# Layer norm, attention with one key head, and a gate, on one core: statistics of one token tile on ScalarE, and an instruction order recorded anew

## The chip, the core and the metric

The kernel runs on one core of a Trainium2 chip. Its engines run their own instruction streams side by side and wait for one another through semaphores: TensorE (PE, with its weight loads shown apart as PEld), VectorE (DVE), ScalarE (ACT), GpSimd (POOL) and SyncE (SP), which here only starts DMAs. TensorE writes to PSUM, a small memory in banks of 128 x 512 fp32; all other data is in SBUF. The metric is the time of one execution on the device in microseconds; a comparison goes by the median of several executions.

## What is computed

For 2048 tokens of width 512, with 32 query heads of width 16 that share one key head and one value head:

```python
xn = (x - mean(x)) / sqrt(var(x) + 1e-5)             # per token
q, k, v = xn @ wq, xn @ wk, xn @ wv                   # 32 heads of 16; one k, one v
s = concat_heads(softmax(q k^T / 4) v) @ wo           # no mask
g = silu(silu(xn @ w1) @ w2)                          # 512 -> 1792 -> 512
out = x + s * g
```

The largest part is the softmax: 32 heads x 2048 x 2048 scores, each of which needs an exponential.

## The kernel before

**Tiles and blocks.** Tokens are cut into 16 tiles of 128 and four chunks of 512. The attention is cut into 32 groups: a group is one chunk of 512 queries and four heads. In a group there are 16 key tiles, and for each key tile four score blocks (one a head) of 128 keys x 512 queries; in all 32 x 16 x 4 = 2048 blocks. A score is a matmul with 16 of the array's rows in use (32 by place), so up to four heads' blocks run side by side in "row" mode; the value products, the projections and the dense layers run in "column" mode, four matmuls of 32 columns side by side (a "quad").

**Two ways to an exponential.** ScalarE takes two blocks at once: scores go to one of two double banks (`psA`), one `Exp` over 128 x 1024 reads them and writes `pa_sb` (line 601), and each block then needs one value product into `psO` (line 723). VectorE takes single blocks from three banks (two halves of `psD`, and `psF`): it makes the bit pattern of a bf16 power of two by adding an offset and rounding to int16 (`ph_sb`, line 639), and GpSimd adds two further offsets to it as packed 64-bit integers (line 664), so that three weighted value products together are near the exponential. A free part of `x_sb` serves as a fourth buffer for these, which is why rows with `x_sb<-psD` are the same work. A block on VectorE so costs three value products where one on ScalarE costs one. The gates' `Tanh` (line 1039) is ScalarE's as well; the group's normalisation (lines 794 to 821), the evacuations of projections and the dense layer are VectorE's.

**The order.** Nothing is ordered by hand after the front. A recorder, class `Sched`, runs when the kernel is built: `op` appends an instruction to an engine's queue, works out its semaphore waits from the keys that it reads and writes, and keeps a model of each engine's clock from costs given with the operations (an operation on GpSimd or VectorE without a cost counts as 0.4 us). The main loop asks that model at each step what to issue next: it fills the time before ScalarE's next pair of scores is needed with value products (`emit_PV`), projection and dense jobs (`emit_job`, bank `psF`, by due times), the front's remaining work (`emit_front`) or zero matmuls that keep TensorE busy (`filler`), and then issues the pair (`score_run`) with single blocks for VectorE beside it (`fill_D`). `advance_v` orders VectorE's tasks. The loop's numbers (how late a bank may come free, how many quads ahead, the share of activity under which fillers are put in, how many buffers may be held) are chosen by stretch: the model's time of ScalarE, divided into stretches of 12 us, picks a letter of `PLAN`, and the letter a row of `RULES`. So a changed cost or rule in one place reorders everything that comes after it.

**The front.** Tiles 0 to 3 are loaded first: 0 and 2 by SP's queue, 1 and 3 by ScalarE's, then wk, a part of wq, tiles 4 to 7, the rest of wq, wv, and the other tiles on SP. While 15 zero matmuls run, VectorE makes statistics of the four tiles (`stats`, line 379, one `bn_stats` each) and aggregates them to mean and variance (`aggr`, line 382). ScalarE takes the square root (`rstd_sqrt`, line 393) and loads the exponential's table; VectorE takes the reciprocal and normalises. Transposes, the first part of the keys and the first queries follow, and the first scores. For the later chunks GpSimd makes the reciprocal root (`rstd_pow`, lines 386 and 388). Two lines of it:

```python
        for t in tiles(0):
            stats(t)
```

**The end.** The last group is done in two halves of 256 queries, then come the last projection, the gate and the last stores.

Of the kernel before, what the change touches and what calls it, by code (L numbers as in the profile page):

```python
# [5 lines left out]
ACT = mybir.ActivationFunctionType  # L6
ALU = mybir.AluOpType
AX = mybir.AxisListType
FP32 = mybir.dt.float32
# [4 lines left out]
P = 128  # L14
DH = 16
NQ = 512
# [180 lines left out]
def bass_recurrent_scan__grouped_kv_mqa__dense_activation_silu__prompt_kernel(  # L197
# [13 lines left out]
    S, D = xf.shape  # L211
    F = B_w1.shape[1]
# [9 lines left out]
    NPA = 11  # L222
# [4 lines left out]
    NWARM = 15  # L227
    NWARM2 = 0
    NWARM3 = 2
    NFRONT = 12  # L230
    AGE2, AGE_ST, FIRST, FRONT_D, FRONT_K, SHORT, ST_EARLY, Q_ACT = 12.0, 1.5, 9.4, 1, 4, 0, 3, 1
    KEEP, ENDQ, ROUND, MAXJOB, AHEAD, Q_EARLY = 0.65, 12, 3.0, 2, 3, 0.18
    LEAD, LEAD_END, SLIP, AGE, AGE1, MARGIN = 3, 1, 0.2, 2.0, 1.2, 0.0
    HALF_LO, HALF_HI = 1, 3
    EV = "vava"
    PVWAIT, FKEEP = 0.2, 0.75
    NPAIR, LEAD_PAIR = 1, 1


    STRETCH = 12.0  # L240
    PLAN = (
        "AAAOFFAAJFNIAOEJAAGAKAALBACLAMFGKLFPNLFANFAEAAAQHAAODBA"
    )
    RULES = dict(
        A=(0.2, 3.0, 0.65, 10, 1.2, 2.0, 0, 12, 0.2, 3, 3, 0.0),
        B=(0.1, 3.0, 0.65, 10, 1.2, 2.0, 0, 12, 0.2, 3, 3, 0.0),
        C=(0.15, 3.0, 0.65, 10, 1.2, 2.0, 0, 12, 0.2, 3, 3, 0.0),
        D=(0.3, 3.0, 0.65, 10, 1.2, 2.0, 0, 12, 0.2, 3, 3, 0.0),
        E=(0.2, 3.0, 0.65, 11, 1.2, 2.0, 0, 12, 0.2, 3, 3, 0.0),
        F=(0.2, 3.0, 0.65, 10, 1.2, 2.0, 4, 12, 0.2, 3, 3, 0.0),  # L250
        G=(0.2, 3.0, 0.65, 10, 1.2, 2.0, 8, 12, 0.2, 3, 3, 0.0),
        H=(0.2, 3.0, 0.65, 10, 1.2, 2.0, 0, 24, 0.2, 3, 3, 0.0),
        I=(0.2, 3.0, 0.65, 7, 1.2, 2.0, 8, 12, 0.1, 3, 3, 0.0),
        J=(0.25, 3.0, 0.65, 8, 1.2, 2.0, 4, 12, 0.2, 3, 3, 0.0),
        K=(0.2, 3.0, 0.65, 7, 1.2, 2.0, -4, 12, 0.2, 3, 3, 0.04),
        L=(0.2, 3.0, 0.65, 10, 2.0, 3.0, 0, 12, 0.2, 3, 3, 0.04),
        M=(0.1, 3.0, 0.65, 10, 2.0, 3.0, 0, 12, 0.2, 3, 3, 0.0),
        N=(0.2, 3.0, 0.65, 10, 1.2, 1.0, 8, 12, 0.2, 3, 3, 0.04),
        O=(0.15, 3.0, 0.5, 10, 1.2, 2.0, 0, 12, 0.2, 2, 3, 0.0),
        P=(0.3, 3.0, 0.7, 10, 1.2, 2.0, 0, 6, 0.2, 3, 3, 0.0),  # L260
        Q=(0.25, 3.0, 0.65, 9, 1.2, 2.0, 0, 12, 0.2, 4, 3, 0.0),
    )
    NF, F_FROM, F_LEFT, F_LATE, DENSE_END, HOLD, F_BEHIND = 14, 0.05, 9, 3, 0.97, 10, 0

    with ExitStack() as es:
        def sb(name, shape, dt=BF16):
            return es.enter_context(nc.sbuf_tensor(name, shape, dt))

        x_sb = sb("x_sb", [P, NT, D])
        xn_sb = sb("xn_sb", [P, 8, D])  # L270
        on_sb = xn_sb
        xnT_sb = sb("xnT_sb", [P, NDC, S])
        wq_sb = sb("wq_sb", [P, NDC, D])
# [15 lines left out]
        t_sb = sb("t_sb", [P, 2, NQ])  # L289
# [6 lines left out]
        mv_sb = sb("mv_sb", [P, NT, 2], FP32)  # L296
# [41 lines left out]
        for j in range(NPH + 1):  # L338
# [11 lines left out]
        op("gp", lambda e: e.tensor_copy(wkp4[:, :, :, 0:DH], wkn_sb[:, :, :].unsqueeze(2).to_broadcast([P, NDC, 4, DH])),  # L350
           reads=["wkn", "wkp"], writes=["wkp"])

        def load_w1():
            op("sp", lambda e: e.dma_start(w1_sb[:], B_w1.rearrange("(dc p) f -> p dc f", p=P)), writes=["w1"], lane="lw1", cost=7.0)

# [19 lines left out]
        def tiles(c):  # L375
            return range(4 * c, 4 * c + 4)
# [7 lines left out]
        def rstd_pow(c):  # L384
            sl = slice(4 * c, 4 * c + 4)
            op("gp", lambda e: e.tensor_scalar(rstd_sb[:, sl], mv_sb[:, sl, 1], LN_EPS, None, op0=ALU.add),
               reads=[("mv", t) for t in tiles(c)], writes=[("rstd", c)])
            op("gp", lambda e: e.tensor_tensor(rstd_sb[:, sl], rstd_sb[:, sl], mhalf_sb[:, :], ALU.pow),  # L388
               reads=[("rstd", c), "mhalf"], writes=[("rstd", c)])

        def rstd_sqrt(c):
            sl = slice(4 * c, 4 * c + 4)
# [105 lines left out]
                   cost=0.155 + (b - a) * P / 960)  # L498

        warm(NWARM, psF[:, :], "F")  # L500
        for t in tiles(0):
            stats(t)
        for t in tiles(0):
            aggr(t)
        rstd_sqrt(0)
        for t in tiles(0):
# [79 lines left out]
        def held(key):  # L586
            return any(p["key"] == key for q in pend for p in q)
# [564 lines left out]
        def needed():  # L1152

            return K.act_end - 0.685 - MARGIN
# [47 lines left out]
        def target(t):  # L1202


            rel, need = max(release(), t), needed()
            if need <= rel:
                return rel
            used = [b for b in dst["fifo"]]
            idle = K.free["v"] + sum(0.6 for b in used)
            frees = [K.ready("pe", [], [b]) for b in BANKS if hold[b] is None]  # L1210
            f = min(frees) if frees else K.free["v"] + 0.65
            x = max(f, idle - 0.43)
            return min(max(rel, x), need) if x <= need + SLIP else need

        def score_run(t):
# [27 lines left out]
            if second:  # L1243
                ast["tile"] = None

        def fill_D(t, free):

            banks = sorted(free_banks(t + SLIP), key=lambda b: (b == "F", K.ready("pe", [], [b])))
            keep = 0
            if "F" in banks and jobs and behind(F_BEHIND) and next_job(t):  # L1250
# [36 lines left out]
        K.free["a"] = max(K.free["a"], FIRST - 0.3)  # L1287
        now, gp_end = 0.0, False
        while state["g"] < NGRP or front or jobs or jst["open"] or tasks:
            (SLIP, ROUND, KEEP, HOLD, AGES["gn1"], AGE, F_BEHIND, ENDQ, PVWAIT, LEAD, AHEAD, MARGIN) = \  # L1290
                RULES[PLAN[min(int(K.act_end / STRETCH), len(PLAN) - 1)]]
            t = max(now, min(K.pe_next("col"), K.pe_next("full")))
            if t > 2000.0:
                raise ValueError(f"the order does not end {state} {jobs[:3]} {jst} {tasks} {dst} {ast}")
# [45 lines left out]
            if more and not blocked:  # L1340
                idle = slots - did
                if idle > 0 and K.activity(max(t, K.pe_last + K.pe_len) + 0.216 * idle) < (FKEEP if front else KEEP):
                    filler(idle)
                score_run(t)
                now = 0.0
            elif not did:
                if dst["open"]:
                    fill_D(t, [0, 1, 2, 3])
                now = t + 0.05
            else:  # L1350
                now = 0.0
# [96 lines left out]
```

## Time and profile before

| | us |
|---|---|
| median of 3 executions | 671.5 (671.2 to 671.59) |
| the profiled execution | 673.14 |
| its span, first to last instruction | 670.3 |
| ScalarE busy | 657.9 (98%) |
| TensorE busy (matmuls) | 649.2 (97%) |
| VectorE busy | 599.9 (90%) |
| GpSimd busy | 375.0 (56%) |
| first `Exp` of scores starts | 10.59 |
| last `Exp` of scores ends | 663.1 |
| `Exp` of scores on ScalarE | 669, 1202 ns each, overlapping |
| blocks on VectorE | 710 (2048 less 2 x 669) |

A group of instructions is given as line, engine, operation, tile written and tile read, shapes, and count; then busy time, the mean in ns of one, and the idle time of the engine just before them with what ended most of it. Neighbouring instructions of an engine overlap, so a mean can be longer than the pace. The chain is the work that ended last, followed back from the last instruction to whatever released it. A row of the windows gives a stretch of time, the busy time and count of each engine, the granted clock of TensorE as a share of the full one, and the share and rate of DMA.

### The profile page before, as it was taken

To read this page: it belongs to the slowest core of one execution; us is meant where nothing else is said; L and a number is where in the kernel's file an instruction comes from. 1 tells how busy PE (TensorE), PEld (TensorE's weight loads), DVE (VectorE), ACT (ScalarE), POOL (GpSimd) and SP (SyncE) were. 2 spreads that over 40 slices of the span, in tenths; PEclk is the share of its full clock that TensorE was granted. 3 is DMA by queue.
4 is the path that set the end of the run, shared out by engine and by line. 5 is a ranking of instruction groups with operands and counts; after the bars stand their busy time and mean duration, and the time that the engine had idled before them with its cause. 6 is when DMAs were issued, how large, how long until landed. Compare 5 with 4: busy or idle time off the path is not lost.

```text
span 670.3 us, 18577 instructions
## 1 busy us (share of the span) xinstructions
PE 649.2 (97%) x8137; PEld 182.2 (27%) x8143; DVE 599.9 (90%) x1008; ACT 657.9 (98%) x755; POOL 375.0 (56%) x379
## 2 busy tenths in 40 slices
PE   8999999999999999999999999999999999999997
PEld 4422222222222222222222222222222222222222
DVE  7899889898888988999899889898899889888997
ACT  6999999999999999999999999999999999999997
POOL 3156546465565655555665566564565547656652
PEclk9999999899999999999999999999999999999999
DMA  6340000000000001000000000010000000000110
GB/s 174 139 147 1 2 2 1 2 1 2 2 1 2 1 18 34 17 2 2 1 2 2 1 2 2 1 34 17 18 2 1 2 2 1 2 2 1 34 33 31
DMA packets 12336, 12.48 MB, mean 19 GB/s; under 512 B 2528, under 2 KB 11744, under 8 KB 12256
## 3 DMA queue, kind: packets, MB, share of 16 engines
q1 hardware_dynamic: 11680, 10.78, 5.2%
q8 instruction: 63, 1.03, 0.6%
q10 hardware_dynamic: 576, 0.52, 0.2%
q14 instruction: 17, 0.14, 0.1%
HBM read 8.95 MB, written 2.10 MB: 16 GB/s over the span
## 4 chain that ended last, share of the span: by engine, by line
ACT 77%; PE 16%; DVE 6%; POOL 1%; DMA 0%; issue 0%; ACTq 0%
ACT pa_sb L601 72%; PE psA L571 5%; PE psO L723 5%; ACT t_sb L1039 5%; PE psF L363 4%; DVE ph_sb L639 1%; DVE stats_sb L379 1%; DVE xn_sb L400 1%; POOL rstd_sb L388 0%; PE psD L571 0%; DVE x_sb L639 0%; DMA x_sb<-in_A_x_dram 0%; PE psD L411 0%; DVE onb_sb L811 0%; PE psD L442 0%
## 5 line engine op out<-in xcount | busy, mean ns | idle before, releaser
L601 ACT ACTIVATE pa_sb<-psA 128x1024 bf16<-128x1024 f32 x669 | 636.5, 1202 | 3.2 <-PE psA L571 1.7
L664 POOL INT64_ADD ph_sb<-ph_sb x292 | 302.3, 1048 | 214.6 <-DVE ph_sb L639 214.4
L639 DVE TENSOR_SCALAR ph_sb<-psD 128x512 int16<-128x512 f32 x513 | 349.5, 692 | 40.1 <-PE psD L571 32.7
L723 PE MATMUL psO<-ph_sb,vaug_sb 128*32 128x512 bf16 x1758 | 218.3, 385 | 0.3
L723 PE MATMUL psO<-pa_sb,vaug_sb 128*32 128x512 bf16 (+1 forms) x1346 | 202.8, 383 | 0.6 <-DVE onb_sb L835 0.6
L571 PE MATMUL psA<-qT_sb,kTa_sb 32*128 32x512 bf16 x680 | 131.9, 384 | 4.5 <-ACT pa_sb L601 3.1
L571 PE MATMUL psA<-qT_sb,kTb_sb 32*128 32x512 bf16 x650 | 126.5, 386 | 7.0 <-ACT pa_sb L601 6.3
L571 PE MATMUL psD<-qT_sb,kTb_sb 32*128 32x512 bf16 x325 | 119.5, 385 | 1.0 <-DVE ph_sb L639 1.0
L571 PE MATMUL psD<-qT_sb,kTa_sb 32*128 32x512 bf16 x311 | 114.0, 384 | 0.0
L664 POOL INT64_ADD x_sb<-x_sb x62 | 64.3, 1049 | 44.9 <-DVE x_sb L639 44.9
L639 DVE TENSOR_SCALAR x_sb<-psD 128x512 int16<-128x512 f32 (+1 forms) x110 | 75.5, 691 | 11.7 <-PE psD L571 10.9
L571 PEld LDWEIGHTS psA<-qT_sb,kTa_sb 32*128 32x128 bf16 x680 | 32.0, 91 | 145.1 <-ACT pa_sb L601 131.2
L571 PEld LDWEIGHTS psA<-qT_sb,kTb_sb 32*128 32x128 bf16 x650 | 30.6, 91 | 144.7 <-ACT pa_sb L601 132.3
L363 PE MATMUL psF<-xnT_sb,w_sb 128*32 128x512 bf16 x896 | 69.6, 386 | 0.0
L363 PE MATMUL psF<-w_sb,u_sb 128*32 128x512 bf16 x896 | 69.2, 384 | 0.0
L723 PEld LDWEIGHTS psO<-ph_sb,vaug_sb 128*32 128x32 bf16 x1758 | 53.9, 95 | 51.2 <-issue 35.3
L723 PE MATMUL psO<-x_sb,vaug_sb 128*32 128x512 bf16 x372 | 65.9, 383 | 0.0
L723 PEld LDWEIGHTS psO<-pa_sb,vaug_sb 128*32 128x32 bf16 x1346 | 49.3, 95 | 43.5 <-issue 34.8
L1039 ACT ACTIVATE t_sb<-psF 128x512 bf16<-128x512 f32 x72 | 56.2, 781 | 0.0
L1071 DVE SCALAR_TENSOR_TENSOR u_sb<-t_sb,psF 128x512 bf16<-128x512 bf16 x56 | 38.2, 682 | 4.8 <-ACT t_sb L1039 3.6
L639 DVE TENSOR_SCALAR ph_sb<-psF 128x512 int16<-128x512 f32 x62 | 42.1, 680 | 0.0
L571 PEld LDWEIGHTS psD<-qT_sb,kTb_sb 32*128 32x128 bf16 x325 | 28.2, 91 | 2.4 <-DVE ph_sb L639 1.4
(125 smaller groups left out, 361.7 us busy)
## 6 DMA issues: line engine op xcount, KB each, us to landing
w_sb<-in_B_w_dram SPq DMA_DIRECT2D x2, 1792.0 KB, 8.9
x_sb<-in_A_x_dram SPq DMA_DIRECT2D x18, 128.0 KB, 2.3
out_dram<-ob_sb SPq DMA_DIRECT2D x14, 128.0 KB, 1.7
x_sb<-in_A_x_dram SPq DMA_DIRECT2D x3, 512.0 KB, 6.5
wop_sb<-in_A_wo_dram SPq DMA_DIRECT2D x1, 512.0 KB, 4.2
wq_sb<-in_A_wq_dram SPq DMA_DIRECT2D x1, 384.0 KB, 6.2
x_sb<-in_A_x_dram ACTq DMA_DIRECT2D x2, 128.0 KB, 2.8
kTb_sb<-kTa_sb SPq DMA_DIRECT2D x16, 16.0 KB, 1.8
```

The costliest lines, as they stand in the source:

```text
L363: r = e.matmul(bank[32 * i:32 * i + 32, :], lhsT=lhsT[:, 32 * i:32 * i + 32], rhs=rhs, start=start, stop=stop, tile_position=(0, 32 * i), ...
L379: op("v", lambda e: e.bn_stats(stats_sb[:, t, :], x_sb[:, t, :]), reads=[("x", t)], writes=[("st", t)], cost=0.687)
L400: op(eng, lambda e: e.tensor_scalar(xn_sb[:, t % 8, :], x_sb[:, t, :], mv_sb[:, t, 0:1], rstd_sb[:, t:t + 1], op0=ALU.subtract, op1=ALU.mult),
L571: return e.matmul(ap, lhsT=kT_sb[g % 2][32 * i:32 * i + 32, kt * P:(kt + 1) * P], rhs=qT_sb[32 * i:32 * i + 32, c % 2, g // 2, :], start=T ...
L601: d = op("a", lambda e: e.activation(pa_sb[:, sl, :], psA[k][:, :], ACT.Exp, scale=ESCALE), reads=["A%d" % k], writes=[("pa", sl)], cost=2 ...
L639: d = op("v", lambda e: e.tensor_scalar(ph_ap(0, sl, 512 * pos, 512 * pos + m), src, float(PH_ONE + PH_BIAS), 0.0, op0=ALU.add, op1=ALU.ma ...
L664: d = op("gp", lambda e, j=j: e.int64_add(ph_ap(j, sl, 0, 4 * NQ).bitcast(I64), ph_ap(0, sl, 0, 4 * NQ).bitcast(I64), PH_SHIFT[j] * 0x0001 ...
L723: r = e.matmul(psO[32 * i:32 * i + 32, cs], lhsT=vaug_sb[:, p["v"], p["kt"], :], rhs=p["ap"], start=s0, stop=s1, tile_position=(0, 32 * i) ...
L1039: op("a", lambda e: e.activation(t_sb[:, n % 2, :], bank_ap(b), ACT.Tanh, scale=0.5 if jb[0] == "h" else 0.25), reads=[b], writes=[("t", n ...
L1071: op("v", lambda e: e.scalar_tensor_tensor(out=dst, in0=t_sb[:, n % 2, :], scalar=1.0, in1=src, op0=ALU.add, op1=ALU.mult), reads=tk["read ...
```

## The change

Three things are changed.

The statistics of tile 1 go to ScalarE. `stats_act` first issues a square root of a constant, then a copy of the tile scaled by 1/512 whose sum is the mean, then a small copy that scales the mean by 512 to the power -1/2, then a square of (mean - x) scaled alike, whose sum is the variance. The other three tiles stay on VectorE.

The recorder is given 0.3 and 1.07 us for the two GpSimd operations of `rstd_pow` in place of 0.4 each.

The numbers per stretch are chosen anew: another `PLAN` (56 letters in place of 55), other `RULES` with two more columns, the letter now picked 0.35 us ahead, and `NFRONT` 16 in place of 12, which sets from what progress on projection and dense jobs are due. The two new columns are `AIM`, until now a fixed 0.43 in `target`, and `XGAIN`: where it is below 2, `extra_fill` runs after each `score_run` and issues one more block for VectorE if a bank comes free within 0.3 us and VectorE would by the model be spared more idle time than `XGAIN` plus the wait. It is below 2 in the letters I, J, K, O and R, which stand in 14 of the 56 places.

```diff
-    NFRONT = 12
+    NFRONT = 16
...
+    XHOLD, XTASK, XWAIT, XGAIN, XCOST, XOPEN, XBEH, AIM = 7, 0, 0.3, 9, 1.0, 0, 99, 0.43
...
-    STRETCH = 12.0
+    STRETCH, AHEAD_BY = 12.0, 0.35
     PLAN = (
-        "AAAOFFAAJFNIAOEJAAGAKAALBACLAMFGKLFPNLFANFAEAAAQHAAODBA"
+        "AAAJFHIPQRACARAAREKMLBPAHAOQDMDJAAJKHQGGQOFIRNIQFGGEMBBA"
     )
     RULES = dict(
-        A=(0.2, 3.0, 0.65, 10, 1.2, 2.0, 0, 12, 0.2, 3, 3, 0.0),
...
+        A=(0.2, 3.0, 0.65, 10, 1.2, 2.0, 0, 12, 0.2, 3, 3, 0.0, 9, 0.43),
...
+        J=(0.2, 3.0, 0.65, 10, 1.2, 2.0, 0, 12, 0.2, 3, 3, 0.0, 0.25, 0.43),
...
+        def stats_act(t):
+
+            r = D ** -0.5
+            op("a", lambda e: e.activation(scr_sb[:, 1:2], eps_sb[:, 0:1], ACT.Sqrt), reads=["eps"], writes=["scr1"], cost=4)
+            op("a", lambda e: e.activation(t_sb[:, 0, :], x_sb[:, t, :], ACT.Copy, scale=1.0 / D, accum_out=mv_sb[:, t, 0:1]),
+               reads=[("x", t)], writes=[("t", 0), ("mean", t)], cost=NQ)
+            op("a", lambda e: e.activation(nm_sb[:, 0:1], mv_sb[:, t, 0:1], ACT.Copy, scale=r), reads=[("mean", t)],
+               writes=["nm"], cost=4)
+            op("a", lambda e: e.activation(t_sb[:, 1, :], x_sb[:, t, :], ACT.Square, scale=-r, bias=nm_sb[:, 0:1],
+                                           accum_out=mv_sb[:, t, 1:2]),
+               reads=[("x", t), "nm"], writes=[("t", 1), ("mv", t)], cost=NQ)
...
-               reads=[("mv", t) for t in tiles(c)], writes=[("rstd", c)])
+               reads=[("mv", t) for t in tiles(c)], writes=[("rstd", c)], cost=0.3)
...
-               reads=[("rstd", c), "mhalf"], writes=[("rstd", c)])
+               reads=[("rstd", c), "mhalf"], writes=[("rstd", c)], cost=1.07)
...
-        for t in tiles(0):
+        stats_act(1)
+        for t in (0, 2, 3):
             stats(t)
-        for t in tiles(0):
+        for t in (0, 2, 3):
             aggr(t)
...
-            x = max(f, idle - 0.43)
+            x = max(f, idle - AIM)
...
+        def extra_fill():
+
+            t = K.pe_last + K.pe_len
+            if sum(held(("pa", k)) for k in range(NPA)) >= XHOLD or group_A() >= NGRP or (XOPEN and jst["open"]) or (XBEH < 99 and behind(XBEH)):
+                return
+            advance_v(t + 0.05)
+            vfree = K.free["v"] + 0.62 * len(dst["fifo"]) + sum(tk["cost"] for tk in tasks if XTASK and all(n in tok for n in tk["need"]) and K.ready("v", tk["reads"], tk["writes"]) < t + 0.6)
+            ride = max(needed(), t + 0.2) + 0.43
+            best = None
+            for b in BANKS:
+                if hold[b] is None and (b != "F" or not jobs or not behind(F_BEHIND) or not next_job(t)):
+                    r = max(t, K.ready("pe", [], [b]))
+                    gain = max(vfree, ride) - max(vfree, r + 0.43)
+                    if r <= t + XWAIT and gain > XGAIN + XCOST * (r - t):
+                        if best is None or r < best[0]:
+                            best = (r, b)
+            if best is None:
+                return
+            fill_D(best[0], [0, 1, 2, 3], [best[1]])
...
-        def fill_D(t, free):
+        def fill_D(t, free, only=None):
...
+            if only:
+                banks = only
...
-                RULES[PLAN[min(int(K.act_end / STRETCH), len(PLAN) - 1)]]
+                RULES[PLAN[min(int((K.act_end + AHEAD_BY) / STRETCH), len(PLAN) - 1)]]
...
                 score_run(t)
+                if XGAIN < 2:
+                    extra_fill()
```

More of the change, by code (lines that the diff above doesn't have):

```diff
@@ L237, in bass_recurrent_scan__grouped_kv_mqa__dense_activation_silu__prompt_kernel @@
     NPAIR, LEAD_PAIR = 1, 1
-    STRETCH = 12.0
+    XHOLD, XTASK, XWAIT, XGAIN, XCOST, XOPEN, XBEH, AIM = 7, 0, 0.3, 9, 1.0, 0, 99, 0.43
+    STRETCH, AHEAD_BY = 12.0, 0.35
     PLAN = (
-        "AAAOFFAAJFNIAOEJAAGAKAALBACLAMFGKLFPNLFANFAEAAAQHAAODBA"
+        "AAAJFHIPQRACARAAREKMLBPAHAOQDMDJAAJKHQGGQOFIRNIQFGGEMBBA"
     )
     RULES = dict(
-        A=(0.2, 3.0, 0.65, 10, 1.2, 2.0, 0, 12, 0.2, 3, 3, 0.0),
[L246 to L261, printed above, removed]
@@ new lines, in bass_recurrent_scan__grouped_kv_mqa__dense_activation_silu__prompt_kernel @@
+        A=(0.2, 3.0, 0.65, 10, 1.2, 2.0, 0, 12, 0.2, 3, 3, 0.0, 9, 0.43),
+        B=(0.1, 3.0, 0.65, 10, 1.2, 2.0, 0, 12, 0.2, 3, 3, 0.0, 9, 0.43),
+        C=(0.2, 3.0, 0.7, 10, 1.2, 2.0, 0, 12, 0.2, 3, 3, 0.0, 9, 0.43),
+        D=(0.2, 3.0, 0.65, 8, 1.2, 2.0, 0, 12, 0.2, 3, 3, 0.0, 9, 0.43),
+        E=(0.2, 3.0, 0.65, 11, 1.2, 2.0, 0, 12, 0.2, 3, 3, 0.0, 9, 0.43),
+        F=(0.2, 3.0, 0.65, 10, 1.2, 2.0, 4, 12, 0.2, 3, 3, 0.0, 9, 0.43),
+        G=(0.2, 3.0, 0.65, 10, 1.2, 2.0, 8, 12, 0.2, 3, 3, 0.0, 9, 0.43),
@@ new lines, in bass_recurrent_scan__grouped_kv_mqa__dense_activation_silu__prompt_kernel @@
+        H=(0.2, 3.0, 0.65, 10, 1.2, 2.0, 0, 12, 0.2, 3, 3, 0.04, 9, 0.43),
+        I=(0.2, 3.0, 0.65, 10, 1.2, 2.0, 0, 12, 0.2, 3, 3, 0.0, 0.15, 0.43),
+        J=(0.2, 3.0, 0.65, 10, 1.2, 2.0, 0, 12, 0.2, 3, 3, 0.0, 0.25, 0.43),
+        K=(0.2, 3.0, 0.65, 10, 1.2, 2.0, 0, 12, 0.2, 3, 3, 0.0, 0.35, 0.43),
+        L=(0.3, 2.5, 0.65, 10, 1.2, 2.0, -8, 12, 0.2, 3, 3, 0.0, 9, 0.43),
+        M=(0.2, 3.0, 0.65, 10, 1.2, 2.0, 0, 12, 0.2, 2, 2, 0.0, 9, 0.7),
+        N=(0.2, 2.75, 0.7, 10, 1.2, 2.0, 0, 12, 0.3, 3, 3, 0.0, 9, 0.43),
@@ L262, in bass_recurrent_scan__grouped_kv_mqa__dense_activation_silu__prompt_kernel @@
+        O=(0.2, 2.75, 0.65, 10, 1.2, 2.0, 0, 12, 0.2, 4, 3, 0.0, 0.05, 0.43),
+        P=(0.2, 3.5, 0.65, 10, 1.2, 2.0, 0, 12, 0.1, 3, 3, 0.04, 9, 0.43),
+        Q=(0.2, 3.0, 0.65, 10, 1.2, 2.0, 8, 12, 0.3, 3, 4, 0.0, 9, 0.43),
+        R=(0.2, 3.0, 0.5, 10, 1.2, 1.5, 0, 12, 0.2, 3, 3, 0.0, 0.35, 0.43),
     )
@@ L270, in bass_recurrent_scan__grouped_kv_mqa__dense_activation_silu__prompt_kernel @@
         xn_sb = sb("xn_sb", [P, 8, D])
+        nm_sb = sb("nm_sb", [P, 1], FP32)
         on_sb = xn_sb
@@ L1244, in score_run @@
                 ast["tile"] = None
-        def fill_D(t, free):
+        def extra_fill():
[17 more added lines that the diff above has]
+        def fill_D(t, free, only=None):
             banks = sorted(free_banks(t + SLIP), key=lambda b: (b == "F", K.ready("pe", [], [b])))
+            if only:
+                banks = only
             keep = 0
-            if "F" in banks and jobs and behind(F_BEHIND) and next_job(t):
+            if not only and "F" in banks and jobs and behind(F_BEHIND) and next_job(t):
                 keep = 1
@@ L1289, in bass_recurrent_scan__grouped_kv_mqa__dense_activation_silu__prompt_kernel @@
         while state["g"] < NGRP or front or jobs or jst["open"] or tasks:
-            (SLIP, ROUND, KEEP, HOLD, AGES["gn1"], AGE, F_BEHIND, ENDQ, PVWAIT, LEAD, AHEAD, MARGIN) = \
-                RULES[PLAN[min(int(K.act_end / STRETCH), len(PLAN) - 1)]]
+            (SLIP, ROUND, KEEP, HOLD, AGES["gn1"], AGE, F_BEHIND, ENDQ, PVWAIT, LEAD, AHEAD, MARGIN, XGAIN, AIM) = \
+                RULES[PLAN[min(int((K.act_end + AHEAD_BY) / STRETCH), len(PLAN) - 1)]]
             t = max(now, min(K.pe_next("col"), K.pe_next("full")))
```

## The prediction

> **What bounds the kernel now.** I read the page first: busy shares, then the costliest groups.
>
> ```profile
> PE 649.2 (97%) x8137; PEld 182.2 (27%) x8143; DVE 599.9 (90%) x1008; ACT 657.9 (98%) x755; POOL 375.0 (56%) x379
> ...
> L601 ACT ACTIVATE pa_sb<-psA 128x1024 bf16<-128x1024 f32 x669 | 636.5, 1202 | 3.2 <-PE psA L571 1.7
> L639 DVE TENSOR_SCALAR ph_sb<-psD 128x512 int16<-128x512 f32 x513 | 349.5, 692 | 40.1 <-PE psD L571 32.7
> L1039 ACT ACTIVATE t_sb<-psF 128x512 bf16<-128x512 f32 x72 | 56.2, 781 | 0.0
> ```
>
> ScalarE's 669 exponentials of two blocks each, idle for only 3.2 us, are the bound; VectorE, which takes the other score blocks, is idle in front of one group for 40.1 us. An exponential's 1202 ns is not its price, since neighbours overlap. The price is in the chain that ended last, here for 60 to 72 us:
>
> ```profile
> 59.57 3.67 ACT pa_sb L601 x4
> 63.24 0.49 ACT t_sb L1039
> 63.73 6.42 ACT pa_sb L601 x7
> ```
>
> 3.67 / 4 = 0.917 us for an exponential, 0.49 for a tanh. The span (670.3) is then: first exponential at 10.59, 669 x 0.917 = 613.5, 72 x 0.49 = 35.3, a tail of 7.1 (the last exponential ends at 663.1 in the timeline), and 3.8 for stalls: 2.4 idle after the first exponential, 1.4 of overlap lost. So time can come out of four places only: the start, the number of exponentials, the 3.8, the tail. The start, in the timeline (start, length, engine, work):
>
> ```profile
> 3.18 2.47 DVE L379 BATCH_NORM_STATS2 stats_sb<-x_sb 128x6 f32<-128x512 bf16 x4 [1.77 <-DMA x_sb<-in_A_x_dram]
> 5.57 0.37 DVE L382 BATCH_NORM_AGGREGATE mv_sb<-stats_sb 128x2 f32<-128x6 f32 x4
> 5.97 0.30 ACT L393 ACTIVATE rstd_sb<-mv_sb,eps_sb 128x4 f32<-128x4 f32 x1 [3.04 <-DVE mv_sb L382]
> 6.28 1.28 ACT L395 ACT_TABLE_LOAD   x1
> 8.48 2.46 DVE L379 BATCH_NORM_STATS2 stats_sb<-x_sb 128x6 f32<-128x512 bf16 x4
> 11.66 1.06 POOL L388 TENSOR_TENSOR rstd_sb<-rstd_sb,mhalf_sb 128x4 f32<-128x4 f32 x1
> ```
>
> Four statistics stand one behind the other on VectorE while ScalarE waits 3.04 us for them. Next, what VectorE waits for over the run (total, times, longest):
>
> ```profile
> DVE ph_sb L639 <- PE psD L571: 32.7, 128, 0.8
> DVE x_sb L639 <- PE psD L571: 10.9, 42, 0.7
> ...
> DVE xn_sb L400 <- POOL rstd_sb L388: 2.0, 3, 0.9
> ```
>
> 170 waits of 0.26 us on average for score blocks. Last, the one large stall of the steady part, in windows of 1 us (PE busy, PEld, DVE, ACT, POOL, then the granted clock):
>
> ```profile
> 121.00:122.00 1.00, 0.60 (x8) 0.29 (x8) 1.00 (x3) 1.00 (x2) 0.00 (x0) 1.00 0.00 0
> 122.00:123.00 1.00, 0.61 (x7) 0.10 (x3) 1.00 (x3) 1.00 (x3) 0.86 (x1) 1.00 0.00 0
> 125.00:126.00 1.00, 1.00 (x11) 0.10 (x3) 1.00 (x4) 1.00 (x3) 0.16 (x1) 0.50 0.00 0
> 127.00:128.00 1.00, 1.00 (x15) 0.21 (x7) 0.55 (x1) 0.33 (x1) 0.98 (x1) 0.66 0.00 0
> ```
>
> TensorE was 60% busy for two microseconds, its clock was then granted at half for some 3.4 us, and ScalarE stood for 0.95 us.
>
> **The change part by part.**
>
> *Statistics of tile 1 on ScalarE.* Removed from VectorE: one statistic (2.47 / 4 = 0.617 us of pace) and one aggregation (0.29 / 4 = 0.07, by the chain's 0.29 for four). VectorE's order is now tiles 0, 2, 3. Tile 2 was issued at 1.15 and landed 2.7 later by the DMA view, at 3.85; VectorE would be free at 3.80. So: tile 0 at 3.18, tile 2 at 3.88, then 2 x 0.617 to 5.11, three aggregations to 5.33, square root at 5.36 instead of 5.97: 0.61 earlier. ScalarE's side: tile 1, issued on its own queue at 0.72, lands 2.6 later, at about 3.36. The square root put first only warms the table: the load already stands at 1.65, before any data. Copy with sum: the 128x512 copy row is 0.597, to 3.98. The scaled mean, by the 128x1 row 0.206, to 4.21 with a hop of 0.03. The square by the copy row plus 0.09 for its bias operand (0.297 of the 128x4 row with bias, less 0.206): to 4.93. Reading out a sum has no row: from nothing to one small activation (0.206) each, so ScalarE ends between 4.93 and 5.35, and the root starts between 5.36 and 5.38. I take 0.61. ScalarE's queue holds nothing else there but the two loads of x, which stay ahead; the added waits on its own results have only the square root behind them.
>
> What moves with it: root, load, reciprocal, normalising, transposes and evacuations all follow the root, so the first exponential goes from 10.59 to 9.98. The warming matmuls end at 6.36 (1.17 + 5.19), the first transposes would start at 6.37. The second chunk gains less: its x, issued at 2.65, lands 5.4 later at 8.06, and statistics that started at 8.48 can't start at 7.87; they gain 0.42. The difference, 0.2, is cover between the second chunk's keys (first half evacuated at 16.46) and the exponential at 17.56 that needs them. Kept as loss: 0 to 0.2; I take 0, since 0.6 us of cover is left. Front: -0.6.
>
> *GpSimd's real times in the recorder.* No instruction changes; the recorder had 0.4 and 0.4 for the two steps whose rows say 0.24 and 1.04, so it thought `rstd` 0.5 early, and VectorE stood at `xn` for 2.0 us in three waits. With the right times it can place a score block there: at 0.617 a block between none and three, so 0 to 1.5 exponentials.
>
> *Extra blocks and new rules.* `extra_fill` starts one more score block where it would remove VectorE idle time; it is open in 14 of 56 stretches (those whose rule has a limit of 0.35 or less). In these windows the profile has VectorE busy 150.55 of 168 us: 17.45 idle, 28 blocks at most. TensorE is the tighter one: busy 165.21 of 168, 2.8 idle, plus a quarter of the fillers (124 matmuls, 31 quads of 0.22, so 1.7). Each exponential moved (two blocks) shortens the run by 0.917 of TensorE's time; it adds four value products (three per VectorE block instead of one: 2130 products for 710 blocks), 0.22, and takes away about as much in a score pair. 4.5 / 0.92 = 5 exponentials at most. The lower end: the other 42 stretches are reordered too, and nothing in the trace excludes loss; a clock halving is the nearest row, 1.0 us. A mean gap (0.26) is less than half a block, so most gaps stay unusable and I take a value near the lower middle: two exponentials fewer with the GpSimd term included, 2 x 0.917 = -1.8. The stalls (3.8, the halving among them) I leave as they are: the order is new everywhere, so 124 us may heal and another place fall. `NFRONT` 16 instead of 12 delays the first projection jobs by four tiles; they are off ScalarE's chain, price nothing while VectorE has idle time, and the queues of SP and POOL keep their order. Tail: same code, 7.1.
>
> Sum: -0.6 - 1.8 = -2.4. The profiled execution took 673.14 (span 670.3 and 2.84 around it), 1.64 over the median of 671.5; it would become 670.7, and the median 669.1. No change can be told within 0.2%, 670.2 to 672.8.
>
> **The rivals.**
>
> *Front only.* The reordering ends with the same number of exponentials: 671.5 - 0.6 = 670.9, within 0.2%. For it: TensorE at 611.3 of 624 us between 36 and 660 leaves little for extra blocks. Against: 44 us of VectorE's waits.
>
> *More halvings of the clock.* More blocks on VectorE and other fillers change where TensorE dips under some two thirds busy for 3 us. Each halving costs 1.0 as at 128 us (0.95 idle and 0.1 of overlap). No exponential gained and two more halvings: 671.5 - 0.6 + 2.1 = 673.0, slower; two is the point from which it decides. For it: one happens in before; nothing in the order prevents it but fillers. Against: only one in 650 us, with TensorE busy 97% of the span. [...]
>
> *A table reload in the front.* If the square isn't in the square root's table, a load of 1.28 goes before it and one before the root: 4.24 + 1.28 + 0.69 + 1.28 + hop, root at 7.5 instead of 5.97, +1.5; with the two exponentials 671.5 + 1.5 - 1.8 = 671.2. For it: root and exponential need a load between them (6.28). Against: copies ran at 7.74 behind that load without another. [...]
>
> **How the numbers follow.** Forecast (front and one to five exponentials net of halvings, 666.8 to 670.1) 0.63, and 669.1; front only 0.18; reload 0.05; halvings or a loss of exponentials 0.14. Faster 0.63; within 0.2% 0.18 + 0.05 = 0.23; slower 0.14. The range runs from four exponentials and a healed stall (671.5 - 0.6 - 3.7 - 0.4 = 666.8) to 672.4, which holds front only, the reload and the first part of the halvings, and leaves about 0.1 on either side.
>
> **What would show it.** Square root at about 5.4 and first exponential at 10.0, with no third table load; 667 exponentials and some 714 blocks on VectorE at 0.917 and 0.62 apart; less VectorE idle behind `psD`; one or no stretch of clock 0.5. Wrong it would be by more ScalarE idle behind `psA` than 3.8, by 669 or more exponentials, or by an exponential group whose pace is over 0.917.

## The result and the profile after

The changed kernel takes 664.57 us (median of 4 executions, 664.45 to 664.87) where the kernel before takes 671.55 in the same comparison: a ratio of 0.9894, 95% interval 0.9879 to 0.9910, so 7.0 us faster. The profiled execution took 664.51, with a span of 662.7. Forecast were 669.1 and at best 666.8.

From the page, the busy shares and the groups that answer to those of before (lines have moved: 601 is now 618, 639 is 656):

```profile
PE 651.1 (98%) x8114; PEld 183.8 (28%) x8114; DVE 598.7 (90%) x1010; ACT 654.5 (99%) x756; POOL 380.0 (57%) x385
...
L618 ACT ACTIVATE pa_sb<-psA 128x1024 bf16<-128x1024 f32 x664 | 631.5, 1202 | 0.8 <-PE psA L588 0.6
L656 DVE TENSOR_SCALAR ph_sb<-psD 128x512 int16<-128x512 f32 (+1 forms) x505 | 343.0, 695 | 33.9 <-PE psD L588 28.4
```

Five exponentials fewer stand on ScalarE, and it waits for almost nothing any more: 0.8 us in place of 3.2, of which 0.6 is before the first one. Their pace is the same 0.917 us (chain pieces of four take 3.67). The span, put together in the same way as in the prediction:

| part of the span, us | before | after | difference |
|---|---|---|---|
| up to the first exponential | 10.59 | 10.07 | -0.52 |
| exponentials, 669 and 664, at 0.917 | 613.5 | 608.9 | -4.6 |
| 72 tanh at 0.49 | 35.3 | 35.3 | 0 |
| stalls and lost overlap (what remains) | 3.8 | 0.7 | -3.1 |
| after the last exponential (663.14 and 654.96) | 7.1 | 7.7 | +0.6 |
| span | 670.3 | 662.7 | -7.6 |

1.05 of the 3.1 is the halving of the clock at 124 us, which not every execution of the kernel before has; the two profiled executions differ by 8.6 us, the medians by 7.0. Between 36 and 650 us TensorE had 12.7 us idle before (614 less 601.29) and has 5.1 after; PE busy comes first in these rows, VectorE (DVE) third:

```profile
36.00:650.00 614.00, 601.29 (x7635) 162.89 (x7635) 555.15 (x901) 612.41 (x702) 358.27 (x346) 1.00 0.04 11
```

```profile
36.00:650.00 614.00, 608.94 (x7677) 165.79 (x7675) 560.76 (x915) 613.94 (x704) 365.51 (x355) 1.00 0.03 10
```

Less idle time on TensorE isn't the gain in itself. Two kernels further down (`searched_all_parts` and `searched_extra_fill_only`) have only 3.1 and 3.8 us of it in the same stretch, and take 670.4 and 676.6 us. Their VectorE is idle for 62.8 and 65.9 us there, against 58.9 before and 53.2 after.

The front in the timeline (ScalarE's and VectorE's rows):

```profile
1.65 1.28 ACT L360 ACT_TABLE_LOAD   x1 [1.65 <-PEq L1474]
...
3.12 2.08 DVE L395 BATCH_NORM_STATS2 stats_sb<-x_sb 128x6 f32<-128x512 bf16 x3 [1.71 <-DMA x_sb<-in_A_x_dram]
3.29 0.63 ACT L361 ACTIVATE t_sb<-x_sb 128x512 bf16<-128x512 bf16 x1
3.82 0.19 ACT L361 ACTIVATION_READ_ACCUMULATOR t_sb<-x_sb 128x1 f32 x1
4.04 0.20 ACT L363 ACTIVATE nm_sb<-mv_sb 128x1 f32<-128x1 f32 x1
4.28 0.72 ACT L365 ACTIVATE t_sb<-x_sb,nm_sb 128x512 bf16<-128x512 bf16 x1
4.91 0.19 ACT L365 ACTIVATION_READ_ACCUMULATOR t_sb<-x_sb,nm_sb 128x1 f32 x1
5.12 0.30 DVE L398 BATCH_NORM_AGGREGATE mv_sb<-stats_sb 128x2 f32<-128x6 f32 x3
5.45 0.30 ACT L409 ACTIVATE rstd_sb<-mv_sb,eps_sb 128x4 f32<-128x4 f32 x1 [0.36 <-DVE mv_sb L398]
```

ScalarE has tile 1 ready at 5.10, VectorE the other three at 5.42: VectorE still sets the start, 0.52 us earlier than before.

To see where the lead comes from, count the blocks done by a given time (two for each exponential of ScalarE that has ended, one for each block of VectorE). By 36 us it is 64 against 56 before, by 156 us 441 against 427, by 300 us 902 against 884, by 492 us 1519 against 1497, by 636 us 1988 against 1960. A block is worth 0.32 us here (653 us for 2048), so of the final lead of 28 blocks 8 are there when the front ends, in stretches whose letter is A in both plans. Some 4 are the halving: the order of before without it, in the run with more zero matmuls below, has 1964 at 636 us. The rest is gathered in small steps forth and back, in stretches with and without `extra_fill`; the largest gain is 7 blocks, from 588 to 600 us, with the letter G, where it isn't open, and the largest loss 6, from 216 to 228 us, with K, where it is.

### The profile page after: what moved, and what is told of

Its sections match the earlier page's. It is cut to its first block, busy times and chain, and to the rows that moved or that the text cites. A ratio compares the mean times of both kernels' runs of the same rounds, so it can differ in the third digit from the quotient of the medians.

```text
span 662.7 us, 18525 instructions
## 1 busy us (share of the span) xinstructions
PE 651.1 (98%) x8114; PEld 183.8 (28%) x8114; DVE 598.7 (90%) x1010; ACT 654.5 (99%) x756; POOL 380.0 (57%) x385
## 4 chain that ended last, share of the span: by engine, by line
ACT 87%; PE 9%; DVE 1%; DMA 1%; SPq 1%; issue 0%; ACTq 0%
ACT pa_sb L618 82%; ACT t_sb L1056 5%; PE psA L588 3%; PE psO L740 3%; PE psF L379 2%; DMA x_sb<-in_A_x_dram 1%; PE psD L427 0%; PE psD L458 0%; DVE stats_sb L395 0%; DMA kTb_sb<-kTa_sb 0%; SPq L476 0%; PE psA L634 0%; DVE kTa_sb L470 0%; PE psD L588 0%; ACT ob_sb L1410 0%
## 5 line engine op out<-in xcount | busy, mean ns | idle before, releaser
L681 POOL INT64_ADD ph_sb<-ph_sb x284 | 293.0, 1044 | 199.9 <-DVE ph_sb L656 199.7
L656 DVE TENSOR_SCALAR ph_sb<-psD 128x512 int16<-128x512 f32 (+1 forms) x505 | 343.0, 695 | 33.9 <-PE psD L588 28.4
L740 PE MATMUL psO<-ph_sb,vaug_sb 128*32 128x512 bf16 x1704 | 212.6, 383 | 0.0
L740 PE MATMUL psO<-pa_sb,vaug_sb 128*32 128x512 bf16 (+1 forms) x1336 | 196.5, 382 | 0.1
L588 PE MATMUL psD<-qT_sb,kTb_sb 32*128 32x512 bf16 x339 | 125.3, 384 | 0.7 <-DMA kTb_sb<-kTa_sb 0.2
L681 POOL INT64_ADD x_sb<-x_sb x76 | 78.7, 1047 | 50.1 <-DVE x_sb L656 50.1
L656 DVE TENSOR_SCALAR x_sb<-psD 128x512 int16<-128x512 f32 x139 | 95.5, 696 | 11.3 <-PE psD L588 10.6
L740 PE MATMUL psO<-x_sb,vaug_sb 128*32 128x512 bf16 x456 | 81.4, 383 | 0.0
L656 DVE TENSOR_SCALAR ph_sb<-psF 128x512 int16<-128x512 f32 x50 | 34.0, 681 | 0.0
```

The costliest lines, as they stand in the source:

```text
L588: return e.matmul(ap, lhsT=kT_sb[g % 2][32 * i:32 * i + 32, kt * P:(kt + 1) * P], rhs=qT_sb[32 * i:32 * i + 32, c % 2, g // 2, :], start=T ...
L656: d = op("v", lambda e: e.tensor_scalar(ph_ap(0, sl, 512 * pos, 512 * pos + m), src, float(PH_ONE + PH_BIAS), 0.0, op0=ALU.add, op1=ALU.ma ...
L681: d = op("gp", lambda e, j=j: e.int64_add(ph_ap(j, sl, 0, 4 * NQ).bitcast(I64), ph_ap(0, sl, 0, 4 * NQ).bitcast(I64), PH_SHIFT[j] * 0x0001 ...
L740: r = e.matmul(psO[32 * i:32 * i + 32, cs], lhsT=vaug_sb[:, p["v"], p["kt"], :], rhs=p["ap"], start=s0, stop=s1, tile_position=(0, 32 * i) ...
```

## The experiments

Theory A: the front is worth its own half microsecond, and the rest is the new order as a whole, made by a plan for one exact sequence of events. Rivals: the front carries more than itself (B) or is eaten by the second chunk (C); the parts add up, with `extra_fill` saving the exponentials stretch by stretch (D).

**The front alone, and the change without the front, in unchanged orders.** The statistics move as in the diff; then the recorder's VectorE clock is set to what the other front would give, so that it records the same order from there on.

```diff
...
-        for t in tiles(0):
+        stats_act(1)
+        for t in (0, 2, 3):
             stats(t)
-        for t in tiles(0):
+        for t in (0, 2, 3):
             aggr(t)
+        K.free["v"] += 1.071
+        K.at[("v", K.done["v"] - 1)] += 1.071
         rstd_sqrt(0)
```

> The kernel before with the statistics of tile 1 on ScalarE and nothing else; the recorder's VectorE clock is put back by hand to what it was, so that every instruction after the front has the order of before (669 exponentials). Theory A (the front is worth its own 0.5 us and no more, the rest of the gain is the new order): the first exponential starts at about 10.1 instead of 10.6 and the time falls by 0.3 to 0.5 us, to about 671.1. Theory B (the front starts the later chunks earlier, and much of the gain follows from it in any order): the time falls by 1.5 us or more. Theory C (VectorE's second chunk, whose x lands at 8.1, eats the start): no change within 0.15 us.

> The changed kernel with the four statistics back on VectorE, and the recorder's clock held so that the order stays that of the changed kernel (664 exponentials). Theory A: 0.5 us slower than the changed kernel, 665.1, the first exponential at 10.6. Theory B: 1.5 us slower or more, since this order was made for the early start and stalls without it. Theory C: the same as the changed kernel.

Measured: 670.75 us against 671.47 (ratio 0.9989, interval 0.9979 to 0.9998), first exponential at 10.12; and 664.96 without the front (0.9896, 0.9881 to 0.9911), 0.4 above the changed kernel, with the first exponential at 10.86 in its profile. In the profiled execution of the first run the last exponential ends 1.51 earlier than before, of which 1.05 is the halving, which this execution didn't have, and 0.47 the start. Over the 18 profiles of this case the first exponential starts at 10.59 to 10.86 us with the old front (8 profiles) and at 10.07 to 10.41 with the new one (10), 0.5 earlier in the mean. So the move of one tile to ScalarE is worth 0.4 to 0.7 us in a given order, by the two pairs of medians. B falls, and so does C as a rule. But an early start can be lost to a late load: in the profile of `searched_front_and_times` below, TensorE waits 0.69 us for wv, and ScalarE, after its first exponential at 10.21, 0.55 us for its second pair of scores.

**The recorder's old costs, and no extra_fill, with the change's plan.**

```diff
-               reads=[("mv", t) for t in tiles(c)], writes=[("rstd", c)], cost=0.3)
+               reads=[("mv", t) for t in tiles(c)], writes=[("rstd", c)])
...
-               reads=[("rstd", c), "mhalf"], writes=[("rstd", c)], cost=1.07)
+               reads=[("rstd", c), "mhalf"], writes=[("rstd", c)])
```

> The changed kernel with the recorder's old cost of 0.4 us for each of the two GpSimd operations; rules, plan and front as changed. The order is recorded again from the first such operation on and comes out with 681 exponentials in place of 664. Theory A (the plan is made for one exact sequence of events, and any disturbance loses it): 17 exponentials more cost 15.6 us, so about 680, slower than before, although only a cost was put back; by 36 us the blocks done, 64 in the changed kernel and 56 before, fall back by 2 to 4, which is what the GpSimd times are worth by themselves. Theory D (the parts add up): 1 to 2 us slower than the changed kernel, 666.

```diff
-                if XGAIN < 2:
+                if False:
                     extra_fill()
```

> The changed kernel with the call of extra_fill taken out; all else as changed. The order comes out with 679 exponentials. Theory A: about 678, slower than before, and the loss doesn't begin where extra_fill is first open but runs through all later stretches. Theory D (extra_fill is what saves the five exponentials, each stretch by itself): five exponentials more, 669, and the blocks done fall back only in the 14 stretches where it is open.

Measured: 683.5 us (1.0173, 1.0155 to 1.0192; 681 exponentials; two executions, 682.7 and 684.3) and 678.8 (1.0104, 1.0085 to 1.0122; 679). Both are far slower than the kernel before, though each only takes one part of the change back. D falls: with a plan that was made for another sequence the recorder loses far more than the part is worth. The run without `extra_fill` has the changed kernel's 64 blocks by 36 us, is 7 blocks behind it by 84 us and 26 by 420.

In the first 36 us, before any letter differs, the runs do tell what the GpSimd times are worth. Waits between 10 and 36 us (total, times, longest), first before, then the changed kernel, then the change without the times:

```profile
DVE xn_sb L400 <- POOL rstd_sb L388: 2.0, 3, 0.9
...
ACT pa_sb L601 <- PE psA L571: 1.5, 5, 0.6
```

```profile
DVE xn_sb L416 <- POOL rstd_sb L404: 0.2, 1, 0.2
...
ACT pa_sb L618 <- PE psA L588: 0.6, 1, 0.6
```

```profile
DVE xn_sb L416 <- POOL rstd_sb L404: 2.0, 3, 0.9
...
ACT pa_sb L618 <- PE psA L588: 1.5, 5, 0.6
```

With the real times the recorder puts statistics and blocks where VectorE would stand waiting for the reciprocal root; the 2.0 us of waiting go, the last chunk's first transposed tiles are evacuated at 27.67 instead of 29.25 (29.78 before), and ScalarE's waits for scores in the front, 0.9 us beyond the start, go with them. Blocks by 36 us: 56 before, 58 with the front alone, 59 with the new front and old times, 63 with the old front and new times, 64 with both. By these counts the times are worth 5 blocks or more, where 2 to 4 were expected, and the front 1 to 3. Of the 5 between the last two kernels with the new front (59 and 64) three are VectorE's, and two are one exponential that ScalarE no longer has to wait for. A count at one instant is rough: two runs below with the same recorder and the same first 44 letters, `no_extra_fill_new_plan` and `searched_front_and_times`, stand at 64 and 61, the latter in the execution with the late load.

**The clock at 124 us.** Two groups of two quads of zero matmuls more, at the two places where TensorE stood idle between score bursts; they take no time in the recorder's model, so the order stays.

```diff
...
+                if 119.8 < t < 120.0 or 121.5 < t < 121.7:
+                    zeros(2)
                 score_run(t)
```

> The kernel before with two groups of two quads of zero matmuls more, added to a finished or running value accumulator at about 120.8 and 122.6 us, where TensorE stood idle between score bursts; they enter the recorder's model at no time, so the order of everything else is that of before. [...]

Windows of 4 us, PE busy first and the granted clock third from the end: the kernel before, the front alone (the same order in these microseconds), and the run with the zero matmuls:

```profile
120.00:124.00 4.00, 2.94 (x37) 0.91 (x33) 4.00 (x8) 4.00 (x6) 1.98 (x3) 1.00 0.00 0
124.00:128.00 4.00, 4.00 (x37) 0.89 (x33) 3.35 (x7) 3.33 (x5) 2.33 (x3) 0.57 0.00 0
```

```profile
120.00:124.00 4.00, 2.94 (x32) 0.80 (x28) 4.00 (x8) 4.00 (x5) 2.05 (x2) 1.00 0.00 0
124.00:128.00 4.00, 3.93 (x55) 1.10 (x52) 4.00 (x9) 4.00 (x6) 2.14 (x2) 1.00 0.00 0
```

```profile
120.00:124.00 4.00, 3.90 (x53) 1.11 (x49) 4.00 (x8) 4.00 (x5) 1.98 (x3) 1.00 0.00 0
124.00:128.00 4.00, 3.94 (x56) 1.10 (x52) 4.00 (x9) 4.00 (x6) 2.36 (x3) 1.00 0.00 0
```

The same 74% busy is followed by half the clock in one execution and by the full clock in another. Expected were no halving near 124 us, a median of about 670.9 and few executions above 672. With the gaps filled, 11 executions lie within 671.08 and 671.54, none above 672, where 7 of 21 executions of the kernel before in this comparison lie above 672 (up to 673.5). Six of these seven have a span of 670.2 to 671.7 us, at a mean granted clock of 0.996 to 0.999; the other one and the remaining 14 have 669.2 to 669.7, as have the 11 (669.3 to 669.7). The median is 671.23, ratio 0.9993 with an interval of 0.9984 to 1.0002, so a lower median isn't shown. The smaller spread rests on 11 executions: over all four comparisons here 25 of 80 executions of the kernel before have a span of 670.2 us or more.

The clock records give the length of the halvings: 3.41 us, in the kernel before from 124.28 to 127.69 at a clock of 0.50. In the 3.41 us ahead of it TensorE was 69% busy (2.35 us).

What decides isn't shown. The prediction's two thirds over 3 us is the one place of the kernel before (1.98 us busy from 121 to 124) and doesn't hold for others: with the front alone TensorE was busy for 1.93 of 3 us from 120 to 123, and for the same 2.94 of 4 us as before from 120 to 124, and kept the full clock. Nor does another threshold come out: the run with the old GpSimd costs was halved after stretches of 3.41 us that were 58 and 69% busy (2.57 of 4 us busy from 348 to 352, clock 0.57 in the next four), while `after_without_extra_fill` (2.37 of 3.41 us, from 450.23) and `searched_rules_only_2` (2.32, from 122.61) kept the full clock. So filling the gaps went with the end of the halvings at this place, and what decides between two stretches that look alike stays open. In the changed kernel's profile the clock is 1.00 throughout.

**One letter for the whole run.** In the changed kernel, and likewise in the 55 letters of before:

```diff
-        "AAAJFHIPQRACARAAREKMLBPAHAOQDMDJAAJKHQGGQOFIRNIQFGGEMBBA"
+        "AAAAAAAAAAAAAAAAAAAAAAAAAAAAAAAAAAAAAAAAAAAAAAAAAAAAAAAA"
```

> The kernel before with the letter A in all 55 places of the plan: one set of numbers for the whole run. The order comes out with 676 exponentials, seven more than before. Theory A: about 678 us. This gives what the choice per stretch was worth in the kernel before, 6 to 7 us.

> The changed kernel with the letter A in all 56 places: the new front, GpSimd's real times, NFRONT 16, no extra_fill, and no choice per stretch. The order comes out with 678 exponentials. Theory A (front, times and NFRONT give nothing lasting by themselves; the gain is in the choice of numbers): about 678, the same as before with one rule within 2 us, and slower than before. Theory D (the parts add up and the choice gives the rest): at least 3 us faster than before with one rule, 675 or less.

Measured: 677.1 us (1.0081, 1.0063 to 1.0100; 676 exponentials) and 678.3 (1.0098, 1.0080 to 1.0117; 678). The choice per stretch is worth 5.6 us in the kernel before and 13.7 in the changed one. Without it the change loses what its front gave: its lead over before with one rule is 8 blocks at 36 us and 4 at 348, and at 636 it is 2 behind.

**Each part with a plan of its own.** If a plan only suits its own sequence, parts must be compared with plans made for each. First one by the blocks done alone:

> The changed kernel without the call of extra_fill, but with a plan of letters searched for this recorder (stretch by stretch, by the blocks that the recorder counts done), in place of the plan that was made for the recorder with it. The order comes out with 668 exponentials, where the same recorder with the old plan has 679. Theory A: about 668.5 us, ten below the run without extra_fill and with the old plan, and faster than before; the loss there was the plan's, not extra_fill's. Theory D: extra_fill is needed, and it stays at 675 or more.

Measured: 671.28 (0.9994, 0.9984 to 1.0003): the last exponential ends 3.0 us earlier than in the profile of before (660.16), but 9.4 us follow it instead of 7.1. Of the 3.0, 1.05 are again the halving. The search had left the end out: value products of the last group had been put off. The time is 7.6 us below the run with the old plan (11 exponentials fewer), where ten were expected, and not faster than before; for the next ones the last twelve letters were chosen by the recorded end. All of them use the changed kernel's table and `NFRONT` with a new `PLAN`; the diffs are those above.

> First of four kernels whose plans were each searched anew with the same method and the same effort (stretch by stretch, eight plans kept, by the blocks that the recorder counts done, then the last twelve letters by the recorded end), so that no part is judged with a plan made for another. All four have the changed kernel's table of numbers and NFRONT 16. This one has neither the new front nor GpSimd's times nor extra_fill: 672 exponentials. From the changed kernel's 664.6 with 664 exponentials, at 0.917 each: about 672. Theory F (front and times are worth 2.5 to 4 us in a plan made for them, extra_fill nothing within 2 us): the two kernels with front and times lie at 669 to 670, the two without at 672 to 674. Theory X (extra_fill is worth the five exponentials): the two kernels with it lie 3 us or more below their pairs.

> As the run before, with extra_fill and without the new front and GpSimd's times: 674 exponentials, about 673.8. Theory F: 0 to 2 us slower than the run with rules only. Theory X: 3 us or more faster than it.

> With the new front and GpSimd's times and without extra_fill: 669 exponentials, about 669.2. Theory F: 2.5 to 4 us faster than the run with rules only, and faster than the kernel before, without any extra block. Theory X: the same as the run with rules only within 1 us.

> All parts of the change, and only the plan from our search in place of the change's own: 670 exponentials, about 670. Theory F: 2.5 to 4 us faster than the run with extra_fill only, within 1.5 us of the run with front and times, and some 5 us slower than the changed kernel, whose plan alone makes that difference. Theory X: 3 us faster than the run with front and times.

> The table and NFRONT of the changed kernel, GpSimd's times, the front as before, no extra_fill, a plan searched for it as in the four searched runs: 669 exponentials, 669 to 670 us. Theory T (the times alone carry the 3.6 us, by blocks that VectorE makes while it would wait for the reciprocal root): 669.5 to 670.5, with 62 or more blocks done by 36 us. Theory P (front and times add up, each about half): about 672.

> The same with the new front and the recorder's old GpSimd cost: 670 exponentials, 670 to 671.5 us. Theory T: 0.5 us better than rules only, 673, with no more than 60 blocks done by 36 us. Theory P: about 672. A count of exponentials that leads to 670 to 671 would say that either part makes an equally good plan possible, and that the scatter of the search is of the size of the parts.

> Rules only (neither front nor times nor extra_fill) with a second plan, from a search that keeps six plans in place of eight: 673 exponentials, where the first search gave 672 and 673.7 us. If the scatter of the search is small against the parts: within 1.5 us of 673.7.

> Front and times without extra_fill with a second plan, six kept in place of eight: 670 exponentials, where the first search gave 669 and 670.1 us. If the scatter is small against the parts: within 1.5 us of 670.1, and at least 2 us under both runs of rules only.

| plan searched for | us | ratio to before (95%) | exponentials | blocks by 36 us |
|---|---|---|---|---|
| rules only | 673.73 | 1.0028 (1.0019 to 1.0037) | 672 | 56 |
| rules only, second search | 675.98 | 1.0061 (1.0046 to 1.0076) | 673 | 56 |
| extra_fill only | 676.63 | 1.0067 (1.0050 to 1.0084) | 674 | 56 |
| front only | 671.01 | 0.9991 (0.9980 to 1.0002) | 670 | 59 |
| GpSimd times only | 670.16 | 0.9972 (0.9961 to 0.9983) | 669 | 64 |
| front and times | 670.13 | 0.9969 (0.9958 to 0.9979) | 669 | 61 |
| front and times, second search | 671.37 | 0.9994 (0.9985 to 1.0003) | 670 | 61 |
| all parts | 670.41 | 0.9980 (0.9970 to 0.9990) | 670 | 64 |
| all parts, the change's own plan | 664.57 | 0.9894 (0.9879 to 0.9910) | 664 | 64 |

Two searches for the same kernel differ by 1.2 and 2.3 us. Beyond that, plans for a recorder with the front, the times or both end at 670.1 to 671.4, those with neither at 673.7 to 676.6. Front and times don't add up, against theory P (672 for either), and the front alone came out better than theory T gave it: 671.0, not 673. `extra_fill` shows no gain in either pair (676.63 against 673.73 and 675.98; 670.41 against 670.13 and 671.37), against theory X. The last two rows are the same kernel but for the letters: 5.8 us.

The traces show one price of `extra_fill`. A block for VectorE whose scores start together with a pair's takes TensorE no longer than the pair (the matmuls of both take 0.38 to 0.39 us, side by side), while one that starts without a pair takes a burst of its own. By the matmuls' starts there are 39 such bursts before and 73 after; 98 and 115 in the two searched kernels with `extra_fill`, and 41 or 42 in `searched_rules_only`, `searched_times_only` and `searched_front_and_times`. That this is why it gains nothing there is likely, not tested.

Two limits. All plans searched here use the changed kernel's table and `NFRONT`, so no run prices these alone; with nothing else of the change (rules only) they end above the kernel before, which has its own table and plan. And in the change's own plan `extra_fill` has no price: taking it out costs 14.3 us, the misfit of the plan included. That it gains nothing is shown for the searched plans only.

## Why the prediction was wrong, point by point

- *The bound and its price* held: ScalarE's exponentials at 0.917 us, tanh at 0.49; in all 18 profiles only 0.6 to 4.0 us remain between the first and the last exponential beyond their number and the 72 tanh at these prices.
- *Statistics on ScalarE, -0.6*: right in mechanism; measured -0.52 at the first exponential and 0.4 to 0.7 in the time. The square root went to 5.45 and not 5.36: the aggregations began at 5.12, as summed (5.11), but the three took 0.30 us, not the 0.22 that came of dividing 0.29 by four (the timeline before has 0.37 for four). Luck has a small part: x landed 0.06 us earlier in this execution (3.12 against 3.18). ScalarE's side was ready at 5.10, inside the bounds 4.93 and 5.35: each sum is read out by an instruction of its own, 0.19 us.
- *GpSimd's real times, 0 to 1.5 exponentials*: too small. VectorE's three blocks more by 36 us are the upper end of the term; missed was that the 2.0 us wait also held up the transposes, and with them ScalarE (0.9 us of waits in the front). Together 5 blocks are 1.6 us at 0.32 a block, against 1.4 at most in the term.
- *Extra blocks and new rules, two exponentials fewer* is the term that failed most: five were saved. The price was hung on `extra_fill` and its 14 stretches, with TensorE's 4.5 us there as the limit, up to five. That the count met this limit is chance: `extra_fill` shows no gain in the searched plans, the lead grows outside its stretches too, and the same kernel with other letters has 670 exponentials and takes 670.4 us. The plan as a whole makes the count, 664 to 681 with the same recorder and one part or the letters changed. The sum also had each exponential moved take a score pair's time off TensorE; five pairs fewer came with 29 score bursts more (741 against 712).
- *The stalls I leave as they are* is the second step that failed, by 3.1 us in the profiles: 0.9 in the front, 1.05 at the halving, the rest at places such as 492 us (0.37 idle), where the new order has none. "124 us may heal and another place fall" came out as healing only: TensorE is busier and its clock is full throughout.
- *The tail* is 0.6 longer, not the same. VectorE's first half of the last group waits for value products until 654.67, 0.3 us before the last exponential ends; before it was 662.14, 1.0 before it:

```profile
654.67 0.45 DVE L850 STREAM_TRANSPOSE otr_sb<-psO 128x256 f32<-128x256 f32 x1 [3.69 <-PE psO L740]
```

```profile
662.14 0.45 DVE L833 STREAM_TRANSPOSE otr_sb<-psO 128x256 f32<-128x256 f32 x1 [1.85 <-PE psO L723]
```

- *The rivals*: no table reload came; the timeline has two loads as before (now at 1.65 and 5.76) and the square at 4.28 without one. The trace shows only that the square needs no load beyond the square root's. Further halvings didn't come in the changed kernel, but are real: the run with the old GpSimd costs has two, at 352 and 560 us (mean granted clock 0.995). Front only, in the order of before, gave about what was worked out for it, 0.7 us by the medians and 0.5 by the start, against 0.6.
- *The range* ended at 666.8, four exponentials and a healed stall, and was bounded by a sum of local prices. Reordering has no local price: with the change's parts and numbers kept and one part or the letters taken back, the time went to 678 to 684.

What stays open: why the change's plan is 5.8 us better than the plans that were searched here for the same recorder. A larger search is the plain guess; no run shows it. For it speaks that the searches here also stay above the kernel before with the parts of before (673.7 and 676.0 against 671.9), if with another table. So a part may be worth more, or less, in a plan as good as the change's than in these. Nor did any run beat the changed kernel.

## What to carry to other kernels

When an order is recorded by a model and steered by numbers per stretch, the numbers fit one sequence of events; put any part of it back and compare only with numbers chosen anew, more than once, or the part seems worth far more than it is. Give the model real durations first where engines wait for one another early in the run, since there a wrong one costs a wait on one engine and the stall behind it on another. Look at TensorE's gaps where its busy share falls as it did ahead of 124 us here (2.35 of 3.41 us busy): the clock was halved after that in one profile, and not in another whose TensorE was as busy (2.94 of 4 us in both). Filling the one at 124 us saved nothing in the median, but none of the 11 executions then had the longer span.

## What the runs showed of the hardware that was not expected

- A ScalarE instruction with a sum is followed by a separate read of the sum, 0.19 us, that starts about 0.1 us before the main instruction's end in the profile (3.82 against 3.29 + 0.63).
- The clock was halved for 3.41 us after a stretch of that length with TensorE 69% busy, in one profile and not in another of the same order (2.94 of 4 us busy in both); the cost at 128 us was 0.95 us of ScalarE idle and 0.1 of overlap, and executions of the kernel before have spans of either 669.1 to 669.9 or 670.2 to 671.8 us.
